# Eight units of attention instead of four ahead of the h stage, with the first W pairs among them and three w_out tiles decoded there

## The chip, the cores and the metric

The program runs on one core of one Trainium2 chip. The metric is the device time of the program in microseconds, as the median of several executions. A core has a matrix engine (TensorE, PE in the rows, with its weight loads as PEld), VectorE (DVE), ScalarE (ACT), GpSimd (POOL) and SyncE (SP), which here issues nearly all transfers; each runs its own instructions in a fixed order and waits for the others by semaphores.

## What is computed

```python
def sm_attn(qq, kk, vv):                      # per batch (8) and head (8)
    s = scale * qq @ kk.T                     # k, v: 576 x 64
    a = softmax(s)
    return a @ vv
p_packed = sm_attn(p, k, v)                   # p: 32 x 64, "packed" k and v
x = sm_attn(q, p_packed, p_packed)            # q: 576 x 64
x = x.transpose(0, 2, 1, 3).reshape(4608, 512)
h = x @ w_in                                  # 512 x 2048
g = s * relu(h) ** 2 + b
x2 = g @ w_out                                # 2048 x 512
y = ((x2 @ w1) * (x2 @ w2)) @ w3 @ w_out2     # 512 x 1024, 1024 x 1024, 1024 x 512
```

The weights w_in, w_out, w1, w2, w3 and w_out2 arrive as 64-bit floats, which the kernel decodes to 32 bit on the chip.

## The kernel before

Precision is kept by splitting each fp32 operand into a high and a low part; `mm3` (L84) multiplies by three matmuls (lines L85, L88, L89), and `split` (L76) makes the parts with a copy on ScalarE (L79) and a subtraction on VectorE (L82).

Decoding one 128 x 512 tile of 64-bit weights (class `Decode`, L121) takes one load into one of four raw buffers (L127, `RAWB` = 4), a square on ScalarE (L140) and four VectorE operations (L144, L150, L157, L161). The raw buffer is free again after L157.

The work on k, v and p is cut into 16 units, each of one batch and four heads. For a unit u, `load_k` and `load_v` (L282, L289) bring 576 KB each, into three buffers each; `A_tr` (L327) transposes k in four parts, `B_s1` (L343) makes the scores, `B_sm1` and `B_sm2` the softmax (L352 to L383), `C_tr` (L391) transposes it, `D_mm` (L406, L411) multiplies by v, and `D_ev` (L420, L421) puts the result into `ppT`. The buffer of k is free after the last transpose, that of v after `D_mm`.

The program has these stages. First a loop over units and tiles of w_in: in step i it loads and transposes unit i, does the scores of unit i-1, the softmax of i-2 and the values of i-3, and decodes three of the 16 tiles of w_in; from step 5 on it also works on the five tiles of q of batch 0 (`q_tr` L188, `q_sc` L202, `q_at` L236). Before the change this loop covers `N1` = 4 units. Then come eight steps of `W_pair` (L470), which multiply the results of batches 0 and 1 with w_in, with the rest of the q tiles; the first w_out loads and the stores of decoded w_in (`win_store`, L560) stand among them. Then the h stage begins: 256 steps idx over batch, half of the tokens and 16 blocks f of w_in's columns. `step_h` (6 matmuls of 288 columns, tile hps; relu and squares at L662 to L674) runs two steps ahead of `step_x` (12 matmuls, tiles xps), which takes w_out tile f. In the first 16 steps the kernel decodes w_out tile idx (`wo_dec`) just ahead of `step_x(idx)`.

The units that are not done in the first loop are spread over the h stage by `plan`, four at a time, so that a step gets at most two parts of a unit (`room`): units 4 to 7 from step 4, 8 to 11 behind them, 12 to 15 from step 98. These late parts use the same lines, save that the score softmax has two reductions (L363, L364). At step 46 the results of units 4 to 7 are wanted by `pp_split`. The last stage (w1, w2, w3, w_out2, lines prod and yps) is not touched.

The written order is only the start: a scheduler reorders instructions on each engine when the program is built, except those that are pinned. What stands in the program after that is shown with the change.

Of the kernel before, what the change touches and what calls it, by code (L numbers as in the profile page):

```python
# [22 lines left out]
def fused_kernel(  # L23
# [36 lines left out]
    NTILE = (NS + 1) // 2  # L60
# [3 lines left out]
    FB1 = F1 // P  # L64
# [101 lines left out]
    if True:  # L166
# [88 lines left out]


        NU = B * NG
        N1 = NU // 4
        ctx0 = ExitStack()
        a1 = ctx0.enter_context(pool("a1"))  # L260
        ctx1 = ExitStack()
# [242 lines left out]
        def wo_dec(f):  # L504
            d = wod.pop(f)
            d.square()
            d.bits1(pin=f == 2)
            d.bits2()
            if f >= NW // 2:
                wo_t[f] = sh.tile([P, 2, DM], F32R, tag="sh", name=f"wo{f}", bufs=NW // 2)  # L510
            else:
                wo_t[f] = wop[0].tile([P, 2, DM], F32R, name=f"wo{f}")
            split(wo_t[f][:, 0, :], wo_t[f][:, 1, :], d.f)
# [13 lines left out]
        def next_win():  # L527
            nonlocal nload
            if nload < NW:
                win_load(nload)  # L530
                nload += 1

        def decode_win():
            nonlocal nbit
            next_win()
            if nbit < NW:
                d = wd.pop(nbit)
                d.square()
                d.bits1(out=win_at(nbit).bitcast(I32))
                d.bits2()  # L540
                nbit += 1
# [1 line left out]
        load_k(0)  # L543
        load_p(0, pz_tile())
        next_win()
        next_win()
        load_k(1)
        next_win()
        make_identity(nc, ident)
# [9 lines left out]
            n = stores.pop(0)  # L559
            tc.keep_in_program_order(nc.sync.dma_start(out=win_d[n], in_=win_at(n)))  # L560

        AS = 5

        def q_step(jq, ps, part):
            if part == 0 and 0 <= jq < NTILE:
                q_tr(0, jq, ps("qtp"))
            if part == 1 and 0 <= jq < NTILE:
                q_sc(0, jq, ps("scp"))
                q_sm1(0, jq)
            if part == 2 and 0 <= jq - 1 < NTILE:  # L570
                q_sm2(0, jq - 1)
                q_ev(0, jq - 1, q_at(0, jq - 1, ps("atp")))

        for i in range(N1 + OFF):
            jq = i - AS
# [21 lines left out]
                A_tr(i, 3)  # L597
            if i >= OFF:
                D_ev(i - OFF)
            decode_win()  # L600
            if 2 <= i < N1 + 2:
                C_tr(i - 2, 0)
                C_tr(i - 2, 1)
            q_step(jq, q_ps, 2)
            if 2 <= i < 2 + NTILE:
                load_q(0, i - 2)
        for j in range(NW // 2):
            jq = j + N1 + OFF - AS
            q_step(jq, m_ps, 0)
            wps = q_ps if j % 2 == 0 else kt_ps  # L610
            W_pair(j, [wps("wps") for _ in range(2)])
            q_step(jq, m_ps, 1)
            q_step(jq, m_ps, 2)
            if j < 3:
                wo_load(j)
            elif j > 3:
                win_store()
                win_store()
        ctx0.close()
        ctx1.close()  # L620
        wop[0] = ctx_a.enter_context(pool("wop", "right"))


        ctx2 = ExitStack()
# [200 lines left out]

        def room(step):
            r_ = step % (2 * FB1) - 2
            return 2 - (step in wsteps) - (0 <= r_ < 5 * NTILE and r_ % 5 in (0, 1, 4))

        def plan(us, start):  # L830
            done = {("p", us[0]): start}
# [57 lines left out]
                    at(t, lambda u=u: D_ev(u))  # L889
            return s_  # L890

        end1 = plan(range(N1, N1 + 4), 4)
        end2 = plan(range(N1 + 4, N1 + 8), end1 + 5)
        end3 = plan(range(N1 + 8, NU), max(end2 + 5, 98))
        PPS = (46, 110, 172)
        assert all(e <= p_ for e, p_ in zip((end1, end2, end3), PPS)), (end1, end2, end3)


        def load_wo2(c):
# [30 lines left out]
                      w3T[m, half][:, 1].rearrange("p a b -> p (a b)"), ps)  # L930
        for idx in range(NST):
            n, r = divmod(idx, 2 * FB1)
            if idx + 3 < FB1:
                wo_load(idx + 3)
            for _ in range(2):
                if stores:
                    win_store()
            if idx < FB1:
                wo_dec(idx)
            if n + 1 < B and r == 2:  # L940
                extra = attn2_steps(n + 1)
            if idx in PPS:
# [288 lines left out]
```

## Time and profile before

| | |
|---|---|
| median of three runs | 1491.2 us (1488.91 to 1491.9) |
| profiled execution, its own time | 1486.73 us |
| span of the profiled execution | 1485.0 us |
| PE busy | 1434.2 us, 97% |
| PEld, DVE, ACT busy | 1314.9, 933.1, 674.1 us |
| data moved by DMA | 228.73 MB |

The page of the profile divides the span into 40 slices of 37 us. In the row of PE all slices but the first five show 9 tenths, the first shows 8 and the second 6. In the DMA row the first slice shows 9 tenths and the second 8. So the two ends of the program differ: up to about 91 us the engines wait for each other and for data; after about 160 us PE is busy without a break for hundreds of microseconds. The stage from 91.3 us on is h.

### The profile page before, as it was taken

To read this page: it belongs to the slowest core of one execution; us is meant where nothing else is said; L and a number is where in the kernel's file an instruction comes from. 1 tells how busy PE (TensorE), PEld (TensorE's weight loads), DVE (VectorE), ACT (ScalarE), POOL (GpSimd) and SP (SyncE) were. 2 spreads that over 40 slices of the span, in tenths; PEclk is the share of its full clock that TensorE was granted. 3 is DMA by queue.
4 is the path that set the end of the run, shared out by engine and by line. 5 is a ranking of instruction groups with operands and counts; after the bars stand their busy time and mean duration, and the time that the engine had idled before them with its cause. 6 is when DMAs were issued, how large, how long until landed. Compare 5 with 4: busy or idle time off the path is not lost.

```text
span 1485.0 us, 26189 instructions
## 1 busy us (share of the span) xinstructions
PE 1434.2 (97%) x10152; PEld 1314.9 (89%) x10152; DVE 933.1 (63%) x2078; ACT 674.1 (45%) x1565; POOL 3.5 (0%) x38
## 2 busy tenths in 40 slices
PE   8688999999999999999999999999999999999998
PEld 5268999999999899998899998899999999999997
DVE  5969644565556776658898564667575655756552
ACT  4456655776556775557776552122131211312111
POOL 0000000000000000000000000000000000000000
PEclk9689999999999999999999999999999999999999
DMA  9846331243235462534664551556565655555451
GB/s 249 260 149 194 107 82 47 58 115 95 77 114 159 123 173 79 148 104 145 193 200 157 177 178 44 211 192 242 179 213 173 215 194 170 194 179 188 171 170 43
DMA packets 127324, 228.73 MB, mean 154 GB/s; under 512 B 50912, under 2 KB 89824, under 8 KB 121056
## 3 DMA queue, kind: packets, MB, share of 16 engines
q1 hardware_dynamic: 127200, 227.06, 48.1%
q8 instruction: 80, 1.31, 0.4%
q14 instruction: 44, 0.36, 0.1%
HBM read 182.98 MB, written 44.04 MB: 153 GB/s over the span
## 4 chain that ended last, share of the span: by engine, by line
PE 48%; DMA 2%; DVE 2%; ACT 1%; issue 1%; SPq 0%; ACTq 0%; DVEq 0%
PE prod L85 8%; PE prod L89 8%; PE prod L88 8%; PE yps L88 4%; PE yps L89 4%; PE yps L85 4%; PE xps L85 2%; PE xps L88 2%; PE xps L89 2%; PE w4a L89 1%; PE w4a L85 1%; PE w4a L88 1%; PE hps L85 1%; PE hps L89 1%; PE hps L88 1%
## 5 line engine op out<-in xcount | busy, mean ns | idle before, releaser
L88 PE MATMUL xps<-gl,wo 128*128 128x288 f32 (+1 forms) x1024 | 301.1, 300 | 0.0
L89 PE MATMUL xps<-gh,wo 128*128 128x288 f32 (+1 forms) x1024 | 298.6, 298 | 0.0
L85 PE MATMUL xps<-gh,wo 128*128 128x288 f32 (+1 forms) x1024 | 274.3, 300 | 1.7 <-DVE wo L82 1.0
L85 PE MATMUL prod<-xc,whl 128*128 128x384 f32 x672 | 226.1, 336 | 2.5 <-DVE c L82 2.5
L89 PE MATMUL prod<-xc,whl 128*128 128x384 f32 x672 | 226.4, 337 | 0.0
L88 PE MATMUL prod<-xc,whl 128*128 128x384 f32 x672 | 226.2, 337 | 0.0
L88 PEld LDWEIGHTS xps<-gl,wo 128*128 128x128 f32 x1024 | 193.5, 189 | 4.5 <-issue 2.3
L89 PEld LDWEIGHTS xps<-gh,wo 128*128 128x128 f32 x1024 | 193.7, 189 | 2.4 <-issue 1.4
L85 PEld LDWEIGHTS xps<-gh,wo 128*128 128x128 f32 x1024 | 182.3, 189 | 6.5 <-issue 2.3
L662 ACT ACTIVATE r<-hps 128x288 f32<-128x288 f32 x256 | 104.4, 410 | 129.7 <-PE hps L89 128.3
L85 PE MATMUL hps<-ATh,wpl 128*128 128x288 f32 x512 | 155.8, 304 | 5.6 <-ACT r L662 4.2
L674 DVE TENSOR_TENSOR gl<-r,gh 128x288 fp32r<-128x288 f32 x256 | 115.1, 453 | 73.1 <-ACT gh L671 70.4
L89 PE MATMUL hps<-ATh,wph 128*128 128x288 f32 x512 | 153.8, 300 | 0.0
L88 PE MATMUL hps<-ATl,wph 128*128 128x288 f32 x512 | 153.5, 300 | 0.0
L85 PEld LDWEIGHTS prod<-xc,whl 128*128 128x128 f32 x672 | 126.2, 188 | 9.7 <-issue 2.8
L88 PEld LDWEIGHTS prod<-xc,whl 128*128 128x128 f32 x672 | 126.2, 188 | 8.2
L89 PEld LDWEIGHTS prod<-xc,whl 128*128 128x128 f32 x672 | 126.2, 188 | 0.1
L664 ACT ACTIVATE r<-r 128x288 f32<-128x288 f32 x256 | 112.6, 444 | 11.1 <-DVE gl L674 6.6
L88 PE MATMUL yps<-w,c 128*128 128x512 f32 x288 | 113.9, 396 | 0.0
L85 PE MATMUL yps<-w,c 128*128 128x512 f32 x288 | 113.2, 395 | 0.3 <-DVE c L82 0.3
L89 PE MATMUL yps<-w,c 128*128 128x512 f32 x288 | 113.4, 395 | 0.0
L85 PEld LDWEIGHTS hps<-ATh,wpl 128*128 128x128 f32 x512 | 97.2, 190 | 11.1 <-ACT r L662 6.4
(332 smaller groups left out, 2312.5 us busy)
## 6 DMA issues: line engine op xcount, KB each, us to landing
whl<-whl SPq DMA_DIRECT2D x48, 1792.0 KB, 7.2
raw<-in_moe_w_dram SPq DMA_DIRECT2D x32, 512.0 KB, 4.4
raw<-in_moe_w_out_dram SPq DMA_DIRECT2D x24, 512.0 KB, 4.6
x<-win SPq DMA_DIRECT2D x48, 256.0 KB, 2.7
v<-in_v_dram SPq DMA_DIRECT2D x16, 576.0 KB, 6.3
q<-in_q_dram SPq DMA_DIRECT2D x72, 128.0 KB, 4.4
x<-xst SPq DMA_DIRECT2D x16, 576.0 KB, 3.4
out_dram<-yst SPq DMA_DIRECT2D x72, 128.0 KB, 2.4
```

What stands on the lines that cost most here:

```text
L85: ins = nc.tensor.matmul(ps, wl, xh, start=start, stop=False)
L88: nc.tensor.matmul(ps, wh, xl, start=False, stop=False)
L89: nc.tensor.matmul(ps, wh, xh, start=False, stop=stop)
L662: nc.scalar.activation(r_, ps[:, :HS], AF.Relu)
L664: nc.scalar.activation(r2, r_, AF.Square)
L674: nc.vector.tensor_tensor(out=gl[:, :HS], in0=r2, in1=gh[:, :HS].bitcast(F32), op=ALU.subtract)
```

## The change

`N1` becomes 8, so units 4 to 7 are done in the first loop and only units 8 to 15 remain for the h stage (`plan` from step 20 and from step 98). The loop has eleven steps instead of seven; each decodes two w_in tiles instead of three, so all 16 are decoded by step 7. The second load and transposition of p move into the loop. From step 7 on (`WS`) each step carries two of the eight W pairs, so the separate loop of W pairs is gone. The first three w_out loads are issued in steps 8 to 10, eight w_in stores in steps 9 and 10; behind the loop three more w_out loads stand and the decoding of w_out tiles 0 to 2. In the h stage w_out tile idx+3 is decoded, and idx+6 loaded, at step idx. `room` gives no part of a unit to a step that has W work.

```diff
--- before.py
+++ after.py
@@ -255,7 +255,7 @@
 
 
         NU = B * NG
-        N1 = NU // 4
+        N1 = NU // 2
         ctx0 = ExitStack()
         a1 = ctx0.enter_context(pool("a1"))
         ctx1 = ExitStack()
@@ -504,7 +504,7 @@
         def wo_dec(f):
             d = wod.pop(f)
             d.square()
-            d.bits1(pin=f == 2)
+            d.bits1()
             d.bits2()
             if f >= NW // 2:
                 wo_t[f] = sh.tile([P, 2, DM], F32R, tag="sh", name=f"wo{f}", bufs=NW // 2)
@@ -542,7 +542,6 @@
 
         load_k(0)
         load_p(0, pz_tile())
-        next_win()
         next_win()
         load_k(1)
         next_win()
@@ -559,7 +558,7 @@
             n = stores.pop(0)
             tc.keep_in_program_order(nc.sync.dma_start(out=win_d[n], in_=win_at(n)))
 
-        AS = 5
+        AS, WS = 5, 7
 
         def q_step(jq, ps, part):
             if part == 0 and 0 <= jq < NTILE:
@@ -570,6 +569,10 @@
             if part == 2 and 0 <= jq - 1 < NTILE:
                 q_sm2(0, jq - 1)
                 q_ev(0, jq - 1, q_at(0, jq - 1, ps("atp")))
+
+        def w_pair(j):
+            wps = q_ps if j % 2 == 0 else kt_ps
+            W_pair(j, [wps("wps") for _ in range(2)])
 
         for i in range(N1 + OFF):
             jq = i - AS
@@ -597,28 +600,31 @@
                 A_tr(i, 3)
             if i >= OFF:
                 D_ev(i - OFF)
-            decode_win()
+            if i == 1:
+                load_p(1, pz_tile())
+            if i == 3:
+                p_tr(1, m_ps("ptp"), 2)
+            if i >= WS:
+                w_pair(2 * (i - WS))
             if 2 <= i < N1 + 2:
                 C_tr(i - 2, 0)
                 C_tr(i - 2, 1)
             q_step(jq, q_ps, 2)
+            if i >= WS:
+                w_pair(2 * (i - WS) + 1)
             if 2 <= i < 2 + NTILE:
                 load_q(0, i - 2)
-        for j in range(NW // 2):
-            jq = j + N1 + OFF - AS
-            q_step(jq, m_ps, 0)
-            wps = q_ps if j % 2 == 0 else kt_ps
-            W_pair(j, [wps("wps") for _ in range(2)])
-            q_step(jq, m_ps, 1)
-            q_step(jq, m_ps, 2)
-            if j < 3:
-                wo_load(j)
-            elif j > 3:
-                win_store()
-                win_store()
+            if N1 <= i < N1 + 3:
+                wo_load(i - N1)
+            if i > N1:
+                for _ in range(4):
+                    win_store()
         ctx0.close()
         ctx1.close()
         wop[0] = ctx_a.enter_context(pool("wop", "right"))
+        for f in range(3):
+            wo_load(f + 3)
+            wo_dec(f)
 
 
         ctx2 = ExitStack()
@@ -825,7 +831,7 @@
 
         def room(step):
             r_ = step % (2 * FB1) - 2
-            return 2 - (step in wsteps) - (0 <= r_ < 5 * NTILE and r_ % 5 in (0, 1, 4))
+            return 0 if step in wsteps else 2 - (0 <= r_ < 5 * NTILE and r_ % 5 in (0, 1, 4))
 
         def plan(us, start):
             done = {("p", us[0]): start}
@@ -889,11 +895,10 @@
                     at(t, lambda u=u: D_ev(u))
             return s_
 
-        end1 = plan(range(N1, N1 + 4), 4)
-        end2 = plan(range(N1 + 4, N1 + 8), end1 + 5)
-        end3 = plan(range(N1 + 8, NU), max(end2 + 5, 98))
+        end2 = plan(range(N1, N1 + 4), 20)
+        end3 = plan(range(N1 + 4, NU), max(end2 + 5, 98))
         PPS = (46, 110, 172)
-        assert all(e <= p_ for e, p_ in zip((end1, end2, end3), PPS)), (end1, end2, end3)
+        assert end2 <= PPS[1] and end3 <= PPS[2], (end2, end3)
 
 
         def load_wo2(c):
@@ -930,13 +935,13 @@
                       w3T[m, half][:, 1].rearrange("p a b -> p (a b)"), ps)
         for idx in range(NST):
             n, r = divmod(idx, 2 * FB1)
-            if idx + 3 < FB1:
-                wo_load(idx + 3)
+            if idx + 6 < FB1:
+                wo_load(idx + 6)
             for _ in range(2):
                 if stores:
                     win_store()
-            if idx < FB1:
-                wo_dec(idx)
+            if idx + 3 < FB1:
+                wo_dec(idx + 3)
             if n + 1 < B and r == 2:
                 extra = attn2_steps(n + 1)
             if idx in PPS:
```

What the program then holds, on three engines. SP's queue is the first (transfers in order of issue). Before the change, from a load of q on, through the last tile of w_in (raw_550) to the first of w_out:

```order
L174 DMA q_412<-in_q_dram 64x8x64 x2
L127 DMA raw_450<-in_moe_w_in_dram 128x512
L127 DMA raw_492<-in_moe_w_in_dram 128x512
L127 DMA raw_510<-in_moe_w_in_dram 128x512
L174 DMA q_529<-in_q_dram 64x8x64 x2
L127 DMA raw_550<-in_moe_w_in_dram 128x512
L174 DMA q_611<-in_q_dram 64x8x64 x2
L174 DMA q_686<-in_q_dram 64x8x64 x2
L302 DMA pz_1018<-in_p_dram 128x2x64 x2
L174 DMA q_751<-in_q_dram 64x8x64
L127 DMA raw_795<-in_moe_w_out_dram 128x512
```

With the change, from the k of unit 7 on:

```order
L282 DMA k_624<-in_k_dram 96x4x384
L127 DMA raw_586<-in_moe_w_in_dram 128x512
L174 DMA q_613<-in_q_dram 64x8x64 x2
L289 DMA v_740<-in_v_dram 96x4x384
L127 DMA raw_656<-in_moe_w_in_dram 128x512
L127 DMA raw_710<-in_moe_w_in_dram 128x512
L174 DMA q_737<-in_q_dram 64x8x64 x2
L289 DMA v_872<-in_v_dram 96x4x384
L127 DMA raw_778<-in_moe_w_in_dram 128x512
L127 DMA raw_832<-in_moe_w_in_dram 128x512
L174 DMA q_870<-in_q_dram 64x8x64
L127 DMA raw_1131<-in_moe_w_out_dram 128x512
```

The k and v loads of units 4 to 7 now all stand ahead of the last w_in tile (raw_832); the last three of the eight are seen here.

On VectorE before the change, the last softmax of q (E2_868, which PE transposes just ahead of h) and the first results of h (gh, gl):

```order
L215 TENSOR_TENSOR E2_868<-scp_861,mx2_866 64x256
L82 TENSOR_TENSOR ATl_837<-atp_875,ATh_836 128x2x128
L224 TENSOR_REDUCE mx2_866<-E2_868 64x8
L225 TENSOR_SCALAR mx2_866<-mx2_866 64x8
L226 RECIPROCAL mx2_866<-mx2_866 64x8
L227 TENSOR_TENSOR E2_868<-E2_868,mx2_866 64x256
L82 TENSOR_TENSOR ATl_837<-atp_895,ATh_836 128x2x64
L673 CAST gh_972<-r2_970 128x288
L674 TENSOR_TENSOR gl_973<-r2_970,gh_972 128x288
```

With the change (the last softmax of q is E2_1151), the end of the same stretch:

```order
L82 TENSOR_TENSOR wpl_1268<-wps_1282,wph_1267 128x512
L144 TENSOR_SCALAR x_1440<-raw_1314 128x512
L150 SCALAR_TENSOR_TENSOR x_1393<-raw_1302,x_1393 128x512
L226 RECIPROCAL mx2_1149<-mx2_1149 64x8
L82 TENSOR_TENSOR wo2_1335<-x_1330,wo2_1335 128x512
L82 TENSOR_TENSOR ATl_1119<-atp_1211,ATh_1118 128x2x128
L150 SCALAR_TENSOR_TENSOR x_1440<-raw_1314,x_1440 128x512
L157 SCALAR_TENSOR_TENSOR x_1393<-raw_1302,x_1393 128x512
L227 TENSOR_TENSOR E2_1151<-E2_1151,mx2_1149 64x256
L144 TENSOR_SCALAR x_1483<-raw_1326 128x512
L82 TENSOR_TENSOR wpl_1268<-wps_1261,wph_1267 128x512
L157 SCALAR_TENSOR_TENSOR x_1440<-raw_1314,x_1440 128x512
```

Operations on w_out (tiles x and wo, at L144, L150, L157, L161 and L82) stand between those of the softmax, and fourteen rows, nearly all of such operations, between its last one and the first gh.

PE around the first W pairs (wps) before the change; of the units only the values (pvp) and the result (ppp) of unit 3 are left:

```order
L406 MATMUL pvp_710<-v_415,E1T_675 32x64 x24
L188 MATMUL qtp_614<-ident_116,q_412 128x128 x4
L202 MATMUL scp_631<-ppT_139,qT_619 64x64 x8
L420 MATMUL ppp_737<-ident_116,pvx_735 128x128
L470 MATMUL wps_804<-winx1_147,ppT_139 64x512 x2
L188 MATMUL qtp_689<-ident_116,q_529 128x128 x4
L470 MATMUL wps_805<-winx1_147,ppT_139 64x512 x2
L202 MATMUL scp_696<-ppT_139,qT_694 64x64 x8
L188 MATMUL qtp_753<-ident_116,q_611 128x128 x4
L470 MATMUL wps_882<-winx3_149,ppT_139 64x512 x2
```

With the change:

```order
L470 MATMUL wps_1008<-winx1_147,ppT_139 64x512 x2
L343 MATMUL s1p_1017<-kT_874,pTd_497 32x288 x5
L202 MATMUL scp_916<-ppT_139,qT_899 64x64 x8
L470 MATMUL wps_976<-winx0_146,ppT_139 64x512 x2
L470 MATMUL wps_1009<-winx1_147,ppT_139 64x512 x2
L406 MATMUL pvp_1154<-v_740,E1T_1098 32x64 x12
L420 MATMUL ppp_1083<-ident_116,pvx_1081 128x128
L406 MATMUL pvp_1154<-v_740,E1T_1098 32x64 x12
L470 MATMUL wps_977<-winx0_146,ppT_139 64x512 x2
L391 MATMUL etp_1197<-ident_116,E1_1029 96x128 x3
L470 MATMUL wps_1122<-winx3_149,ppT_139 64x512 x2
L236 MATMUL atp_1003<-ident_116,E2_797 128x128 x2
```

The scores (s1p), transposes (etp) and values (pvp) of units 6 and 7 stand among the first W pairs (wps) and the q tiles.

## Rows read from the trace of the kernel before

**Rows 1.** Stages: span, busy us (count) of PE, PEld, DVE, ACT, POOL; PEclk, DMA share, GB/s
```profile
5.00:47.00 42.00, 32.57 (x365) 20.72 (x366) 27.40 (x63) 19.07 (x43) 0.26 (x6) 0.86 0.99 254
47.00:60.00 13.00, 7.58 (x47) 3.47 (x39) 12.63 (x29) 4.76 (x8) 0.00 (x0) 0.50 0.79 220
60.00:91.30 31.30, 22.46 (x136) 9.29 (x132) 23.49 (x57) 17.28 (x35) 0.00 (x0) 0.83 0.80 267
91.30:130.00 38.70, 36.09 (x267) 33.50 (x266) 30.50 (x70) 23.98 (x59) 1.58 (x16) 0.89 0.51 145
130.00:160.00 30.00, 25.55 (x239) 24.31 (x240) 28.93 (x71) 23.05 (x53) 0.99 (x10) 1.00 0.61 194
200.00:300.00 100.00, 100.00 (x876) 95.43 (x875) 48.19 (x123) 61.90 (x147) 0.00 (x0) 1.00 0.22 59
```

**Rows 2.** DMA issues, first 60 us: count, KB each, median us to landing
```profile
raw<-in_moe_w_in_dram SPq DMA_DIRECT2D x16, 512.0 KB, 7.4
k<-in_k_dram SPq DMA_DIRECT2D x4, 576.0 KB, 11.5
```

**Rows 3.** Timeline from last w_in load to first x: start us, us, engine, line, operation
```profile
52.96 0.55 SPq L127 DMA_DIRECT2D raw<-in_moe_w_in_dram  x1
59.54 0.43 DVE L144 TENSOR_SCALAR winx<-raw 128x512 int32<-128x512 int32 x1
...
91.33 0.61 PE L85 MATMUL hps<-ATh,wpl 128*128 128x288 f32 x1
...
96.50 0.71 PE L85 MATMUL xps<-gh,wo 128*128 128x290 f32 x4
```

**Rows 4.** Timeline, as before: starts of neighbouring instructions on VectorE and TensorE
```profile
66.62 0.41 DVE L224 TENSOR_REDUCE mx<-E 128x8 f32<-128x256 f32 x1
66.95 0.68 DVE L161 SCALAR_TENSOR_TENSOR winx<-m,winx 128x512 f32<-128x512 bf16 x1
...
101.10 0.30 PE L88 MATMUL hps<-ATl,wph 128*128 128x288 f32 x1
101.23 0.29 PE L89 MATMUL hps<-ATh,wph 128*128 128x288 f32 x1
...
104.17 1.28 DVE L157 SCALAR_TENSOR_TENSOR x<-raw,x 128x512 uint32<-128x512 uint32 x2
...
105.01 0.41 PE L327 MATMUL ktp<-ident,k 96*128 96x96 f32 x3
...
105.20 0.38 PE L85 MATMUL hps<-ATh,wpl 128*128 128x288 f32 x1
```

**Rows 5.** Groups on PE, 91.3 to 160 us: count, busy us, mean ns, idle before
```profile
L89 PE MATMUL xps<-gh,wo 128*128 128x290 f32 x64 | 19.6, 308 | 0.0
L89 PE MATMUL hps<-ATh,wph 128*128 128x288 f32 x46 | 14.4, 313 | 0.0
L327 PE MATMUL ktp<-ident,k 96*128 96x96 f32 x24 | 3.2, 250 | 0.0
L343 PE MATMUL s1p<-kT,pTd 64*32 64x288 f32 x16 | 1.4, 415 | 0.0
L406 PE MATMUL pvp<-v,E1T 96*32 96x64 f32 x48 | 1.2, 223 | 0.0
L391 PE MATMUL etp<-ident,E 128*96 128x128 f32 x6 | 1.0, 272 | 0.0
```

**Rows 6.** Waits of SP's queue, first 110 us: us, times, longest
```profile
SPq L127 <- DVE x L157: 18.0, 1, 18.0
SPq L174 <- PE qtp L188: 7.0, 1, 7.0
```

**Rows 7.** DMA issues of the whole program, w_out
```profile
raw<-in_moe_w_out_dram SPq DMA_DIRECT2D x24, 512.0 KB, 4.6
```

**Rows 8.** Waits of the engines, 59.5 to 91.3 us: us, times, longest
```profile
PE atp L236 <- DVE E L227: 3.8, 2, 2.5
ACT m L140 <- DMA raw<-in_moe_w_out_dram: 3.2, 2, 2.3
```


## The prediction

> **What bounds the kernel now.** I read the stages by time first [rows 1]. The reader should look at three of their columns: PE, DVE and the DMA share. From 5 to 47 us the DMA engines are busy 0.99 of the time at 254 GB/s while PE works 32.57 of 42.00 us and VectorE 27.40: transfers set the pace. From 47 to 60 us VectorE does (12.63 of 13.00). From 60 to 91.3 us nobody is full: PE 22.46, VectorE 23.49 of 31.30, TensorE's granted clock 0.83. From 91.3 us, where h begins, to 160 us VectorE is busy 30.50 + 28.93 = 59.4 of 68.7 us and PE loses time to it. By 200 us PE is busy 100.00 of 100.00, and work taken off PE there is time off the end. So the change moves units out of a stretch where PE is the bound into one where transfers are. The question is whether the first grows by less than the second shrinks.
>
> The timeline between the two gives the marks [rows 3]: the last w_in load is issued at 52.96, VectorE takes it up at 59.54, the first matmul of h starts at 91.33 and the first of x at 96.50.
>
> **Term 1: how much later h begins.** Ahead of the last w_in tile SP's queue holds, before, 8 loads of k and v at 576 KB, 16 of w_in at 512 KB [rows 2], 4 of q at 128 KB and 2 of p at 64 KB (sizes of the last two from the code): 13,440 KB. With the change it holds 16 of k and v, 16 of w_in, 8 of q and 4 of p: 18,688 KB. The difference is 5,248 KB or 5.37 MB. At the 254 GB/s of the stretch where the queue is full [rows 1] that is 21.2 us, at 267 GB/s 20.1 and at 220 GB/s 24.4. I take 21.2, the rate of the stretch with the same mix of loads. VectorE takes up the last w_in tile at 59.5 + 21.2 = 80.7 us. In that time VectorE has to do less than there is time for: four units add some ten short operations each and no decode.
>
> What follows the last tile is VectorE's. In the order, 52 rows of it lead from that tile's first operation to the last softmax operation of q, for which PE waits ahead of h. By kind: 25 operations on 512 columns, six L144, ten on about 256 columns, 11 short ones. Starts of neighbours tell what one costs in a full queue [rows 4]: two L157 take 1.28 us together where one takes 0.68, so 0.60 apart; a 256-wide one frees the engine after 0.33 (66.62 to 66.95), which I use for L144 too, and for a short one I estimate 0.2. The sum is 25 x 0.60 + 16 x 0.33 + 11 x 0.2 = 22.5 us. Before, the 58 rows of the same stretch come by the same prices to about 22.4 us, and took 91.3 - 59.5 = 31.8 us. The 9.4 us between are waits, such as PE's for the softmax (3.8) and ScalarE's for a w_out load (3.2) [rows 8], which come when VectorE has run out of other work; its busy 23.49 of 31.30 says so. Now three more w_out tiles stand there to fill such gaps, and six of the eight W pairs need no late tile. I take 1.8 us of waits, between none and 9.4. h begins at 80.7 + 22.5 + 1.8 = 105.0 us, against 91.3: **+13.7 us**.
>
> **Term 2: from the first h to the 160 us mark.** Up to 160 us PE did 3 x (64 + 46) = 330 matmuls of x and h [rows 5]; they start 0.13 apart where nothing holds them (101.10 and 101.23, [rows 4]); with 0.133 that is 43.9 us. Beside them it did parts of late units: two units' k transposes (24), one unit's scores (16), transposes (6) and values (48), and the second transposition of p. One unit's groups are busy 1.6 + 1.4 + 1.2 + 1.0 + about 0.3 (its transposed result) = 5.5 us [rows 5]; but matmuls overlap: after three transposes busy 0.41 us the next matmul starts 0.19 later [rows 4]. So a unit takes between 2.6 us (19 parts in 41 of it) and 5.5. I take 4.3, above the middle, since each change between kinds of matmul costs something too. The second unit's k transposes are 1.6 of 5.5, so 1.3 units were done: 5.6 us, with some 0.5 for p 6.1. The rest of the 68.7 us, 18.7, is q tiles, which stay, and waits.
>
> With the change the units and p go, -6.1 us. Of the waits I take 3.5 us away. The reason is VectorE: a w_out tile is four operations and a split, 4 x 0.60 + 0.33 = 2.7 us, and in the order five of the 16 tiles are finished and three more begun before the first gh, instead of two in all; four fewer tiles are 10.8 us out of 59.4, the units' own operations come on top, and in the first 16 steps VectorE stops being the bound. Against it, the 14 rows between the last softmax and the first gh (ten at 0.60, three at 0.33, 7.1 us) delay the first x: it starts some 7.5 us after the first h instead of 5.2, and PE idles there, since `step_h` is only two steps ahead. This is in the 3.5. **-9.6 us**, from -6 to -14.
>
> **Term 3: the units that no longer come after the mark.** Of units 4 to 7, 4 - 1.3 = 2.7 were done after 160 us, where PE is never idle [rows 1]: 2.7 x 4.3 = **-11.6 us**, from -7.0 to -14.9. VectorE, busy 48.19 of 100 there, covers its share of units 8 to 15 as before, and these only move to earlier or equal steps.
>
> The other edits I cost at nothing. Behind the last w_in tile SP's queue holds, up to the fifth w_out tile, five w_out loads (2.6 MB), eight w_in stores (2.1 MB) and five of q (0.7 MB): 5.4 MB, 20.2 us at the 267 GB/s of that stretch [rows 1]. VectorE wants that tile eight rows (3.5 us) ahead of the stretch's end, 22.5 - 3.5 + 1.8 = 20.8 us after the last w_in tile. So it covers them, but the cover is thin; without it the softmax waits, rival (b). ScalarE's part of an early unit, four copies of k, two of E1T and an exponential, lies beside the transfers (ScalarE 19.07 of 42.00 us). That a loop step decodes two w_in tiles and not three is hidden, since transfers set that pace.
>
> **Sum.** 1486.73 (profiled execution) + 13.7 - 9.6 - 11.6 = 1479.2 us. That execution lies 4.5 us under the median of 1491.2; on the median's footing the change gives **1483.7 us**, -0.5%. A measurement of this kernel can tell about 0.2%, 3 us, from no change.
>
> **Rivals.**
> (a) *The waits of the old tail come back.* The stretch of 31.8 us had 9.4 us of waits. If PE, ScalarE and VectorE hand the last q tiles to each other as slowly as before, h begins 7.6 us later: 1491.3 us, no change. For it: the last softmax chain is serial in both. Against it: VectorE has other work between now.
> (b) *Slower: w_out loads stand in front of the softmax.* Raw buffers are four. The fifth to seventh w_out load can be issued only after L157 of the tile four before, and VectorE's first operation on these tiles stands ahead of the last softmax (raw_1314, the fifth) and of the first gh (raw_1387, the seventh, raw_1434, the eighth). SP waited 18.0 us for such an L157 in one case [rows 6], and a w_out load takes 4.6 us from issue to landing [rows 7]. If each of three such round trips is exposed, 13.8 us are added: 1483.7 + 13.8 = 1497.5 us. It is slower than now by a measurable amount from about 10.5 us on, so two exposed trips (9.2) are not enough. Against it: the raw buffer of the first w_out tile is freed some 10 us before the fifth is wanted.
> The Trainium skill (DMA: Bandwidth & Descriptors, "Anatomy of one DMA") says that a wait of a transfer is spent on the issuing sequencer, so all that is queued behind it waits too; SP's 7.0 us for PE's q transposes [rows 6] agree.
> (c) *More is gained.* If k and v come at 267 GB/s (-1.1), h begins without waits (-1.8) and a unit costs 5.5 us on PE (4 x 1.2 = 4.8), the time is 1483.7 - 7.7 = 1476 us.
> (d) *The loads cost less.* k and v are read in runs of 1,536 bytes (6 x 64 x 4). If such runs moved faster than 254 GB/s and VectorE's decode of w_in had held them back, h would begin up to 8 us earlier and the time would be 1475 us. Against it stands the DMA share of 0.99. The Trainium skill (DMA: Bandwidth & Descriptors, "Specifications") calls 512 bytes enough for line rate and puts HBM's limit per core at about 358 GB/s; by that 5.37 MB would take 15.0 us instead of 21.2 and the sum would be 6 us lower. The row disagrees.
> (e) *It does not do what it says.* The scheduler could have put the units behind h again; the order excludes that, as s1p and pvp of units 6 and 7 stand among the first W pairs.
>
> **Chances.** The forecast, 1478 to 1488: 0.47. (a) 1488.5 to 1494: 0.19. (b) 0.16. (c) 0.14, (d) 0.04, (e) none. Faster by over 0.2% are the forecast, (c) and (d): 0.65; within 0.2% is (a): 0.19; slower is (b): 0.16. The range leaves out the farther half of (b) and the low end of (c) and (d): 1474 to 1496 us.
>
> **What would show it.** In the changed kernel's profile the DMA share should stay near 0.99 to about 78 us, VectorE's first operation on the last w_in tile should lie at 79 to 83 us, the first hps at 103 to 107, the first xps at 110 to 114. From the first h on, VectorE should no longer be over 85% busy, and L327, L343, L391 and L406 should have 48, 64, 24 and 192 fewer instructions behind h. The prediction is wrong if a DMA share well under 0.9 shows before 75 us (SP is held up), if VectorE waits over 5 us between the last w_in tile and the last softmax (a), or if L144 of w_out waits for its load there (b).

## The result, and the profile after

The changed kernel takes 1474.4 us (median of four runs, 1469.3 to 1478.5), the kernel before beside it 1491.0 us (1488.9 to 1491.9). The ratio is 0.989 with a 95% interval of 0.985 to 0.993: 16.6 us faster. The direction was right. The time lies below the 1478 to 1488 us that had the largest chance and just inside the wide range of 1474 to 1496 us; the gain forecast was 7.5 us. The profiled execution of the changed kernel took 1469.31 us, its span is 1467.5 us, 17.5 us under the span of before.

The first view is the one of [rows 1] with the same edges, for the changed kernel (span, busy us and count of PE, PEld, DVE, ACT, POOL; PEclk, DMA share, GB/s):

```profile
5.00:47.00 42.00, 36.69 (x373) 23.46 (x371) 25.55 (x60) 19.75 (x47) 0.00 (x0) 0.84 1.07 251
47.00:60.00 13.00, 10.25 (x137) 6.39 (x138) 8.68 (x27) 7.31 (x19) 0.26 (x6) 0.91 1.09 229
60.00:91.30 31.30, 28.27 (x352) 13.77 (x344) 25.91 (x70) 18.14 (x42) 0.00 (x0) 0.93 1.01 257
91.30:130.00 38.70, 29.30 (x184) 22.67 (x184) 38.70 (x90) 25.64 (x58) 1.17 (x12) 0.87 0.81 260
130.00:160.00 30.00, 30.00 (x249) 29.53 (x248) 27.61 (x67) 22.08 (x53) 1.47 (x14) 1.00 0.53 160
200.00:300.00 100.00, 100.00 (x932) 94.73 (x931) 44.65 (x116) 58.23 (x144) 0.00 (x0) 1.00 0.24 66
```

Against [rows 1], the DMA share stays over 1 up to 91 us, where it had fallen to 0.8 from 47 us on: the loads now set the pace that long. VectorE is busy all the time from 91.3 to 130 us. PE is full from 130 to 160 us, where it had lost 4.45 us.

The timeline of the changed kernel has the marks that answer [rows 3] (start us, us, engine, line, operation):

```profile
83.07 0.37 DVE L144 TENSOR_SCALAR winx<-raw 128x512 int32<-128x512 int32 x1
...
104.93 0.41 DVE L227 TENSOR_TENSOR E<-E,mx 64x256 f32<-64x256 f32 x1
...
108.61 0.27 DVE L82 TENSOR_TENSOR ATl<-atp,ATh 128x128 fp32r<-128x128 f32 x1
...
108.94 0.61 PE L85 MATMUL hps<-ATh,wpl 128*128 128x288 f32 x1 [2.13 <-DVE ATl L82]
...
113.36 0.29 PE L85 MATMUL xps<-gh,wo 128*128 128x290 f32 x1
```

The last w_in tile is taken up at 83.07 us (before 59.54), the first h starts at 108.94 (91.33), the first x at 113.36 (96.50).

Where the 17.5 us come from can be told by counting the matmuls of h and x, 4608 in both kernels, and reading when each number is reached. The table gives the time from one mark to the next, worked out from the records of the two traces; 18 matmuls are a step. Other work can cross a mark (12 W matmuls of steps 49 to 64 run behind matmul 1300 in the changed kernel alone), so single parts say less than the sums.

| part | steps | before | after | difference |
|---|---|---|---|---|
| to the first h | | 91.3 | 108.9 | +17.6 |
| h/x matmuls 1 to 337 | 0 to 19 | 68.7 | 50.6 | -18.1 |
| 337 to 1300 | 19 to 72 | 162.4 | 163.2 | +0.8 |
| 1300 to 2000 | 72 to 111 | 115.9 | 111.9 | -4.0 |
| 2000 to 2500 | 111 to 139 | 93.2 | 84.4 | -8.8 |
| 2500 to 4000 | 139 to 222 | 257.8 | 251.9 | -5.9 |
| 4000 to the end | | 695.7 | 696.5 | +0.8 |

Two things stand out. The first 19 steps gain twice what was forecast, and the rest comes in two places far behind them that the prediction does not name. At both, steps 113 to 128 and 177 to 192, the program computes `W_tile` for later batches ("W stretch" below).

### The profile page after: what moved, and what is told of

It is laid out like the page before. It is cut to its first block, busy times and chain, and to the rows that moved or that the text cites. A ratio compares the mean times of both kernels' runs of the same rounds, so it can differ in the third digit from the quotient of the medians.

```text
span 1467.5 us, 26161 instructions
## 1 busy us (share of the span) xinstructions
PE 1430.7 (97%) x10152; PEld 1310.6 (89%) x10152; DVE 931.2 (63%) x2070; ACT 669.4 (46%) x1557; POOL 3.6 (0%) x38
## 4 chain that ended last, share of the span: by engine, by line
PE 89%; DMA 7%; ACT 2%; DVE 2%; issue 1%; SPq 0%; ACTq 0%; DVEq 0%
PE xps L85 9%; PE xps L88 9%; PE xps L89 9%; PE prod L85 8%; PE prod L88 8%; PE prod L89 8%; PE yps L88 5%; PE yps L89 5%; PE yps L85 5%; PE hps L85 5%; PE hps L89 4%; PE hps L88 4%; DMA raw<-in_moe_w_in_dram 2%; DMA k<-in_k_dram 2%; PE scp L202 1%; PE qtp L188 1%
## 5 line engine op out<-in xcount | busy, mean ns | idle before, releaser
L88 PE MATMUL xps<-gl,wo 128*128 128x288 f32 (+1 forms) x1024 | 297.2, 298 | 0.0
L89 PE MATMUL xps<-gh,wo 128*128 128x288 f32 (+1 forms) x1024 | 295.5, 296 | 0.0
L85 PE MATMUL xps<-gh,wo 128*128 128x288 f32 (+1 forms) x1024 | 263.8, 299 | 0.1
L89 PEld LDWEIGHTS xps<-gh,wo 128*128 128x128 f32 x1024 | 192.9, 189 | 2.2 <-issue 1.4
L85 PEld LDWEIGHTS xps<-gh,wo 128*128 128x128 f32 x1024 | 178.2, 188 | 3.8 <-issue 0.9
```

The costliest lines, as they stand in the source:

```text
L85: ins = nc.tensor.matmul(ps, wl, xh, start=start, stop=False)
L88: nc.tensor.matmul(ps, wh, xl, start=False, stop=False)
L89: nc.tensor.matmul(ps, wh, xh, start=False, stop=stop)
```

## The experiments

All of them were compared with the kernel before on the same chip. A second number helps: from the first h on, kernels with the same order agree closely. The changed kernel took 1358.6 us from the first h to the end in its first trace and 1359.7 in another; before it was 1393.6. The first h itself moves by several microseconds from execution to execution, so this stretch shows more than the median does.

### The changed kernel again

No edit.

> The changed kernel once more, to see which of its gains repeat. In the first pair of profiles it was 17.7 us ahead at the end of the h and x matmuls, but level at h/x matmul 1300 (step 72); the 18 us came at matmuls 2000 to 2500 (W steps 113 to 128, -8.8 us, of which -5.2 us on the wps matmuls) and 3300 to 3500 (W steps 177 to 192, -5.6 us). Theory 'the plan does it': 1470 to 1479 us, and the wps matmuls at steps 113 to 128 again take about 0.23 us from one start to the next (0.33 in the kernel before). Theory 'chance of one execution': the time stays near 1474, but the wps matmuls of one of these stretches take 0.30 us or more in this profile.

Measured: 1476.0 us (1467.7 to 1476.9), ratio 0.989 (0.986 to 0.992). First h at 115.5 us instead of 108.9; from there every part of the table is within 1.1 us of the first trace (84.4 us for matmuls 2000 to 2500, wps 0.23 us apart). The gains behind the first h belong to the program; what changes between executions is when h begins. It goes with the rate of the loads. The windows from 5 to 83 us of the changed kernel in its two traces, and of the kernel without units 12 to 15 (below; same instructions up to h), in this order:

```profile
5.00:83.00 78.00, 67.50 (x772) 40.47 (x770) 51.83 (x136) 40.39 (x97) 0.26 (x6) 0.87 1.08 249
```
```profile
5.00:83.00 78.00, 62.83 (x711) 37.30 (x713) 45.45 (x117) 36.41 (x85) 0.26 (x6) 0.85 1.07 235
```
```profile
5.00:83.00 78.00, 63.94 (x640) 38.89 (x638) 42.33 (x109) 33.87 (x80) 0.26 (x6) 0.75 1.08 223
```

At one and the same DMA share the rate is 249, 235 and 223 GB/s, and the first h starts at 108.9, 115.5 and 120.3 us. From the start of the last VectorE operation on w_in to the first h it is 17.8 us in all three.

### The w_out part alone, and the units alone

The first is the kernel before with the w_out edits only, the second the changed kernel without them.

```diff
 # the kernel before, w_out part alone
-            d.bits1(pin=f == 2)
+            d.bits1()
...
+        for f in range(3):
+            wo_load(f + 3)
+            wo_dec(f)
...
-            if idx + 3 < FB1:
-                wo_load(idx + 3)
+            if idx + 6 < FB1:
+                wo_load(idx + 6)
...
-            if idx < FB1:
-                wo_dec(idx)
+            if idx + 3 < FB1:
+                wo_dec(idx + 3)
```

> The kernel before with the w_out part alone: three w_out tiles decoded ahead of h, the others three steps ahead of x; four units ahead of h as before. My forecast put the waits of VectorE and PE behind h at 3.5 us and the three decodes ahead of h at 15 VectorE rows, 6.5 us. Theory 'the w_out part takes the waits of the first 16 steps': h begins 5 to 8 us later, the first 16 steps lose 8 to 12 us, 1484 to 1489 us. Rival 'the waits are the late units' own': h begins 5 to 8 us later and gets back no more than that, 1490 to 1496 us.

> The changed kernel without the w_out part: eight units ahead of h, but every w_out tile decoded in its own step of x as before. Theory 'w_out takes the waits of the first 16 steps': h begins some 7 us earlier (101 to 103 us), PE waits for the w_out tiles behind it, end 1477 to 1484 us. Rival 'four late units fewer is all of it': h begins 7 us earlier and most of that stays, 1466 to 1473 us.

Measured: the w_out part alone 1492.4 us, ratio 1.002 (1.001 to 1.004); the units alone 1486.9 us, ratio 0.998 (0.996 to 1.000). Neither is worth anything to speak of; together they give 16.6 us. The w_out part alone came out in its rival's range, and yet the waits went, as its other theory has it; the units alone lie outside both ranges.

| | first h | h/x matmuls 1 to 337 | first h to end |
|---|---|---|---|
| before | 91.3 | 68.7 | 1393.6 |
| w_out part alone | 101.6 | 55.3 | 1388.9 |
| units alone | 104.0 | 66.9 | 1373.6 |
| both | 108.9 | 50.6 | 1358.6 |

The windows of these 336 matmuls, for the w_out part alone, the units alone and the changed kernel (the kernel before has, from 91.3 to 160 us, PE 36.09 + 25.55 and VectorE 30.50 + 28.93 busy of 68.7 us, [rows 1]):

```profile
101.60:156.90 55.30, 55.09 (x429) 52.86 (x429) 41.40 (x99) 37.70 (x93) 2.61 (x26) 0.97 0.51 155
```
```profile
104.00:170.90 66.90, 55.02 (x430) 52.49 (x431) 60.14 (x139) 43.24 (x100) 3.11 (x26) 0.97 0.50 156
```
```profile
108.90:159.60 50.70, 50.66 (x401) 49.95 (x402) 48.34 (x111) 37.13 (x88) 2.64 (x26) 0.97 0.60 192
```

With the units alone PE works 6.6 us less than before (55.0 against 61.6), which is close to the 6.1 us of the forecast, but it now stands still for 11.9 us instead of 7.1: VectorE's 60 us of work is there as before, and PE meets it sooner. Who is waited for is in PE's waits of that kernel over the same stretch:

```profile
PE xps L85 <- DVE wo L82: 7.1, 4, 3.2
PE hps L85 <- ACT r L665: 2.6, 2, 1.6
PE scp L202 <- ACT qT L194: 2.2, 1, 2.2
```

The w_out part takes VectorE's work there from 59.4 to 41.4 us, and PE waits no more; but ahead of h it must be done too. In the kernel before the loads of w_in are done by then, and the scheduler put eight w_out tiles ahead of the first h, which fill VectorE (busy 40.33 us of the 41.60 from 60 us to the first h): 10.3 us lost of the 13.4 gained, and of these only 4.7 are left at the end (1393.6 to 1388.9). In the changed kernel VectorE has time ahead of h while the loads run, and the same work costs 4.9 us (104.0 to 108.9) for 16.3 (66.9 to 50.6). Some of these differences of the first h are the loads' own, up to the 6.6 us seen between two traces of one kernel. The trace of the units alone is also that of its fastest execution of ten, 1479.4 us. An estimate by the medians takes from each median the time from the first h to the end and the 1.7 to 2.1 us by which the traced execution is longer than its span: the first h then starts at about 95.7 us before, 101.4 with the w_out part alone, 111.5 with the units alone and 114.0 with both. By this the w_out part costs some 6 us alone and 2 to 3 us beside the units.

### One w_out tile ahead, and three w_in tiles per unit

```diff
 # one tile ahead
-        for f in range(3):
-            wo_load(f + 3)
-            wo_dec(f)
+        wo_load(3)
+        wo_dec(0)
...
-            if idx + 6 < FB1:
-                wo_load(idx + 6)
+            if idx + 4 < FB1:
+                wo_load(idx + 4)
...
-            if idx + 3 < FB1:
-                wo_dec(idx + 3)
+            if idx + 1 < FB1:
+                wo_dec(idx + 1)
```

> The changed kernel with one w_out tile decoded ahead of h and the others one step ahead of x (instead of three and three). Theory 'the lead of one step is what matters, since PE then never meets a tile that is still being decoded': h begins 3 to 4 us earlier than in the changed kernel and the first 16 steps stay full, 1469 to 1474 us. Rival 'the number of decodes left for the first 16 steps matters: VectorE is the bound there': two tiles more, 10 VectorE rows, 4.3 us, come back, 1474 to 1480 us. If one step is too short, PE waits for wo again as it does without the w_out part (16 us more behind h): 1480 us or more.

Measured: 1478.3 us, first h to end 1360.1. The question stays unanswered, since the program hardly differs: the trace has the same 42 VectorE rows, one of them in another place, between the last w_in operation and the first h, three finished w_out tiles among them. The scheduler moves the decodes ahead by itself as far as loads and buffers allow.

```diff
 # three w_in tiles per unit
+            decode_win()
             if i == 1:
                 load_p(1, pz_tile())
```

> The changed kernel with three w_in tiles loaded and decoded per unit ahead of h instead of two, as the kernel before did: the same bytes, but the last w_in tile lands ahead of the k and v of units 6 and 7. Theory 'VectorE's tail behind the last load sets the first h': six VectorE rows (3 to 4 us) move from the tail into the stretch in which VectorE waits for loads, and h begins 3 to 8 us earlier; 1467 to 1473 us. Rival 'the last load sets it, whichever it is, and unit 7's own chain then ends last': within 2 us of the changed kernel, 1473 to 1477 us.

Measured: 1482.1 us (ten runs), some 7 us slower than the changed kernel, where either theory had it faster or level. The last w_in operation did come earlier (86.0 us against 91.2), but between it and the first h (116.1) stand 69 VectorE rows instead of 42: six w_out tiles are finished ahead of h instead of three. From the first h on it takes 1358.5 us, no less. So decodes beyond three ahead of h cost their VectorE time there and give nothing back, as the first 19 steps are full of PE's work already.

### Loads left out

```diff
+            if u > 5:
+                kt[u] = kt[5]
+                return
```

The same lines stand in the load of v; units 6 and 7 then work on the k and v of unit 5.

> The changed kernel without the loads of k and v for units 6 and 7, which take unit 5's tiles instead (so the third and fourth batches' output is not the reference's); every other instruction stays. It takes 4 x 576 KB = 2.36 MB out of the stretch ahead of h, where the DMA engines' share is 1.05 to 1.10 up to 83 us. Theory 'the loads set when h begins, VectorE's tail behind them is a constant': 2.36 MB at 233 to 247 GB/s is 9.6 to 10.1 us; the last w_in row and the first h both come that much earlier for the rate of that execution (after the rate of 247 GB/s at 99 us, after 208 to 221 GB/s at 110), the tail between them stays 17.8 us, and the median falls from 1474 to 1476 us to 1464 to 1467 us. Rival 'VectorE is nearly full there as well and takes over': the first h moves by 4 us or less, the tail grows by 5 us or more, 1470 to 1473 us.

Measured: 1470.3 us (1465.9 to 1474.5), 4 to 6 us less than the changed kernel, the time that the rival gave. Its windows behind 75 us:

```profile
75.00:83.00 8.00, 6.85 (x90) 3.05 (x86) 8.00 (x23) 6.48 (x15) 0.00 (x0) 1.00 0.68 241
83.00:106.80 23.80, 15.47 (x108) 5.38 (x108) 23.80 (x60) 14.40 (x30) 0.00 (x0) 0.83 0.87 265
```

The DMA share has fallen to 0.68 and VectorE is full from 75 us to the first h at 106.8, as the rival has it; but the stretch from the last w_in operation to the first h grew by 1.6 us only (17.8 to 19.4), where the rival had 5 us or more. By how much h itself moved this one trace can't tell, since the first h of the changed kernel lies between 108.9 and 115.5 us. By the medians two units' loads cost 4 to 6 us, not the 10 that their bytes take at the rate of the loads: VectorE's own work hides about half of them.

### What a late unit costs

```diff
-        end3 = plan(range(N1 + 4, NU), max(end2 + 5, 98))
+        end3 = 0
```

What needs `ppT` of batches 6 and 7 reads that of 4 and 5.

> The changed kernel with units 12 to 15 left out: no k, v or p loads, transposes, scores or softmax for them, and what needs their result takes that of units 8 to 11 (so the output of the last two batches is not the reference's). It prices a late unit. Theory 'a late unit costs its own matmuls': 12 ktp, 16 s1p, 6 etp, 48 pvp and 2 more rows are some 3.5 us of PE from start to start each in the changed kernel's trace, my forecast took 4.3: 4 units are 14 to 17 us, so 1457 to 1462 us. Rival 'a late unit costs what the change saved per unit behind the first h (35.3 us for four, 8.8 us each)': 1438 to 1443 us.

Measured: 1454.3 us; the first h came late (120.3 us), and from it to the end it is 1332.8 us, 25.8 less than the changed kernel, or 6.5 us a unit. That is more than the units' own matmuls (from start to start 12 transposes of k take 0.83 us, 16 matmuls of scores 1.24, 6 transposes 0.49, 48 of values 0.81 and the rest 0.1, 3.5 us in all, 14 for four), and less than 8.8. Of the 11.8 us beyond the 14, 9.8 lie between matmuls 3300 and 4000 (111.8 us instead of 121.6), around the third W stretch, where the changed kernel has no part of a unit; some 1.8 us of these 9.8 are six W matmuls and four q transposes that run ahead of matmul 3300 there. The measured price lies between the two theories.

### What crowds a W stretch

Four kernels move the late units about; the first number is where units 8 to 11 begin, the second where 12 to 15 begin (20 and 98 in the changed kernel).

```diff
 # 20 and 106
+        end3 = plan(range(N1 + 4, NU), max(end2 + 5, 106))
 # 45 and 106
+        end2 = plan(range(N1, N1 + 4), 45)
+        end3 = plan(range(N1 + 4, NU), max(end2 + 5, 106))
 # 4 and 45
+        end2 = plan(range(N1, N1 + 4), 4)
+        end3 = plan(range(N1 + 4, NU), max(end2 + 5, 0))
 # 20 and 81
+        end3 = plan(range(N1 + 4, NU), max(end2 + 5, 0))
```

A fifth, 20 and 114, also has the `room` of the kernel before.

> Units 12 to 15 start at step 106 as in the kernel before (not 98), all else as changed; unit 12 then spans steps 106 to 139 across the W steps 113 to 128. Theory 'the place of the third group gives the late gain': most of the 8.8 us of h/x matmuls 2000 to 2500 come back, 1480 to 1486 us. Rival 'the place of the group is worth nothing, only the number of late units counts': 1470 to 1479 us.

> The changed kernel with the third group of units started at step 114, and W steps allowed to take one part of a unit as in the kernel before: unit 12's transposes then stand among the W steps 113 to 128, where the kernel before has them by its trace (ptp and ktp at steps 117 to 122, since its second group runs late, to step 112). Theory 'late units that spill into a W stretch crowd its W matmuls together': the W matmuls begin later than step 119, take 0.30 us or more each instead of 0.23, and h/x matmuls 2000 to 2500 take 89 to 94 us instead of 84.4; 1479 to 1486 us. Rival 'the spill is harmless, the kernel before lost the 9 us by other things': 84 to 86 us there, 1470 to 1478 us.

> The changed kernel with units 8 to 11 started at step 45 and units 12 to 15 at step 106, where the kernel before has them: still four late units fewer, but the second group ends late again (its last ppp stands at step 112 in the kernel before, at 85 in the changed one). The stretch from the first h to the end is compared, since the first h itself moves with the loads from one execution to the next: 1358.6 to 1359.7 us in three traces of the changed kernel, 1393.6 before. Theory 'a group that ends late makes the W stretch behind it start late and crowds its W matmuls': wps of steps 113 to 128 again at 0.33 us or more (0.234 in the changed kernel), h/x matmuls 2000 to 2500 at 92 to 95 us (84.4), first h to end 1366 to 1371 us. Rival 'fewer late units is what opened that stretch': 84 to 86 us there, 1358 to 1362 us.

> The changed kernel with units 8 to 11 started at step 4 and units 12 to 15 right behind them (step 45, last part at step 101), so that no group ends shortly ahead of a W stretch that needs it. Theory 'late ends crowd the W stretches': the third stretch opens too (0.234 us per W matmul instead of 0.312, as in the run with units 12 to 15 left out, where h/x matmuls 3500 to 4608 took 161 us instead of 172), first h to end 1343 to 1353 us. Rival 'VectorE is full in the first 16 steps, and units there cost more than they give back': the first 16 steps take 55 us or more instead of 50.7 and the sum is within 5 us of the changed kernel, 1355 to 1364 us.

> The changed kernel with units 12 to 15 started right behind units 8 to 11 (step 81 instead of 98, last part planned at step 140 instead of 160), units 8 to 11 as changed. Theory 'late ends crowd the W stretches': the last ppp stands at 150 or earlier instead of 172, the third W stretch opens to 0.234 us per W matmul, first h to end 1346 to 1354 us; its rival, that the third stretch is crowded by other work (decodes, q steps), gives 1357 to 1361 us.

Measured medians: 1474.8, 1479.2, 1479.4, 1476.9 and 1472.4 us. By them none clearly beats the changed kernel (20 and 81 has 1466.3 to 1476.4 us, within that kernel's spread); the parts behind the first h say more. For each W stretch the table gives the step at which its first matmul (wps) really starts by the trace, the mean time from the start of one of its 48 wps matmuls to the start of PE's next matmul, and the time of the h/x matmuls around it.

| kernel | second stretch: step, ns, 2000 to 2500 | third: step, ns, 3300 to 4000 | first h to end |
|---|---|---|---|
| before | 124.8, 328, 93.2 us | 189.8, 330, 125.5 us | 1393.6 |
| changed | 119.0, 233, 84.4 | 186.6, 315, 121.6 | 1358.6 |
| 20 and 106 | 116.0, 235, 84.4 | 188.4, 353, 121.8 | 1358.7 |
| 20 and 114 | 116.5, 251, 84.8 | 189.7, 327, 125.8 | 1362.5 |
| 45 and 106 | 122.6, 249, 87.6 | 189.8, 333, 124.2 | 1362.3 |
| 4 and 45 | 126.0, 306, 93.5 | 180.3, 234, 111.8 | 1357.2 |
| 20 and 81 | 126.9, 321, 98.5 | 178.8, 233, 109.6 | 1359.3 |
| without 12 to 15 | 116.5, 236, 81.6 | 180.3, 234, 111.8 | 1332.8 |

Wherever a stretch begins, its last matmul starts within a few steps of the same place, at 135.8 to 139.0 in the second and 200.9 to 204.3 in the third, where the program has h take its results; what differs is when it begins. Begun early it costs 0.23 us a matmul; begun some six steps later, it costs 0.31 to 0.33 us, and PE runs ahead of ScalarE and VectorE, which must split each result. The windows of the second and third stretch show it, first of the kernel before, then of the one with 4 and 45:

```profile
477.40:531.30 53.90, 50.28 (x339) 45.76 (x338) 39.78 (x79) 41.81 (x91) 0.00 (x0) 0.97 0.52 146
681.00:738.40 57.40, 52.25 (x346) 45.58 (x345) 47.73 (x100) 45.83 (x101) 0.00 (x0) 1.00 0.53 164
```
```profile
496.40:548.00 51.60, 46.62 (x318) 41.60 (x315) 38.84 (x78) 40.76 (x89) 0.00 (x0) 1.00 0.48 140
659.00:726.80 67.80, 67.80 (x489) 64.74 (x488) 52.92 (x113) 54.46 (x122) 0.00 (x0) 1.00 0.46 142
```

and of the changed kernel:

```profile
458.20:520.00 61.80, 61.80 (x444) 58.66 (x444) 43.10 (x88) 48.54 (x105) 0.00 (x0) 1.00 0.46 140
657.70:718.90 61.20, 56.40 (x382) 50.19 (x380) 48.40 (x102) 48.38 (x107) 0.00 (x0) 1.00 0.49 154
```

An open stretch keeps PE busy without a gap (61.80 of 61.80, 67.80 of 67.80); a crowded one loses 3.6 to 5.2 us to waits. The granted clock is no rival for this: it is 1.00 in all but one of these windows, and the 0.97 of the second stretch of the kernel before is worth 0.03 of 53.9, 1.6 us, by estimate. In the second stretch of the kernel before it waits for this:

```profile
PE wps L85 <- ACT wpst L462: 2.9, 2, 2.4
PE hps L85 <- DVE wpl L82: 0.7, 1, 0.7
```

Each wps tile is held until ScalarE has copied it (L462), and there are only two such buffers, shared with the late units' parts and the q tiles.

Why a stretch begins late: the units' parts run behind the plan. In the kernel before the second group is planned to end at step 100, and its last result (ppp) stands at step 112 in the trace; the W matmuls planned for 113 begin at 125, as far behind. In the changed kernel the second group is over at step 85, and unit 12, planned to end at 112, ends at 117.7; the stretch begins at 119. Moving both groups early ("4 and 45", "20 and 81") opened the third stretch, as forecast, and crowded the second: units planned without a pause up to step 100 or 112 arrive at the second stretch some 14 steps late again. So the sums missed the forecast (1357.2 and 1359.3 us from the first h on, where 1343 to 1354 were given). "45 and 106" was to crowd the second stretch again, at 0.33 us or more, and did so by little, 0.249 us and 87.6 us, nearer to the rival that fewer late units open it. That their number alone does it is excluded by "4 and 45" and "20 and 81", which have as few as the changed kernel and are crowded there. That starting the third group at 98 instead of 106 gives the gain in the second stretch is excluded by "20 and 106" (84.4 us). That units merely stand among W matmuls is harmless: "20 and 114" has k transposes of unit 12 at steps 122 to 135 and 0.251 us a matmul, with 84.8 us around them. So my theory of that run was wrong: what it loses, it loses in the third stretch (125.8 us), which its later group crowds.

## Why the prediction came out as it did

**Term 1** was +13.7 and measured +17.6 in this pair of traces, with the loads at the upper end of their rates. Up to the last softmax operation it came out, in part by luck: the last w_in tile was taken up at 83.07 against 80.7 us, 2.4 late, but the 22.3 us from there to the end of that operation are the 22.5 of the rows alone, without the 1.8 of waits, so that it ended at 105.3 against 105.0. What failed is the step from there to h. The forecast let h begin with the end of the softmax, as it nearly does before, 0.5 us behind it; here h came 3.6 us behind it, the last 2.1 of them spent waiting for the split of the last transposed q tile (ATl, 108.61), ahead of which VectorE had five w_out operations and one of W to do. The kernel before starts h ahead of that split:

```profile
91.33 0.61 PE L85 MATMUL hps<-ATh,wpl 128*128 128x288 f32 x1
...
91.74 0.29 DVE L82 TENSOR_TENSOR ATl<-atp,ATh 128x128 fp32r<-128x128 f32 x1 [0.92 <-ACT ATh L79]
```

So the first h needs none of that tile's tokens. What it needs is the buffer: in the changed program as built, the first hps gets the PSUM bank (a buffer for results of matmuls) that the transposed tile had, bank 0, and its first matmul waits for that tile's split. In the kernel before that tile is in bank 3, with the units alone in bank 1, and there too h starts ahead of the split (104.00 and 104.15 us). By the medians the first h is 18.3 us later (95.7 to 114.0). Rivals (a) and (b) didn't come true: VectorE had no gap from 91.3 us to the first h. Rival (c), 1476 us, is nearest in time, but the loads didn't run at 267 GB/s and h didn't begin without a wait; only its dearer unit, 5.5 us, points the right way. Rival (d) fell too: with the queue full to 83 us the loads ran at 249 GB/s over that stretch here and slower elsewhere, not faster than the 254 assumed. The Trainium skill (DMA: Bandwidth & Descriptors, "Specifications") has 512 bytes enough for line rate, with some 358 GB/s as HBM's limit for a core; the rows here, with a mix of runs of 1,536 bytes (k, v) and 4 KB (w_in) and a share of 1.07 to 1.08, show 223 to 249 GB/s and disagree.

**Term 2** was -9.6, from -6 to -14, and measured -18.1. The mechanism, waits on VectorE that w_out decodes cause, was right; the term was mis-sized. I took 3.5 us of waits away, and all 7.1 went (PE 50.66 of 50.70 busy). And I counted a unit's parts by their own length, 6.1 us for 1.3 units; from start to start, with the waits that stood behind them, those rows (ktp, etp, s1p, pvp, ppp, ptp) took 10.9 us before and none now. The x and h matmuls took 5.2 us less (52.4 to 47.2), the q tiles' parts 2.0. A part of this is the granted clock, which the forecast left out: it was 0.89 from 91.3 to 130 us before and 0.97 over the 50.7 us after, which by estimate is (1 - 0.89) x 38.7 - (1 - 0.97) x 50.7 = 2.7 us. What I did not see is that units and w_out are not two terms to add: the units alone gave 1.8 us here.

The step that VectorE would "no longer be over 85% busy" was wrong: its work fell by 11.1 us, as worked out (10.8), but the stretch shrank by 18, and it is 95% busy (48.34 of 50.70).

**Term 3** was -11.6, from -7.0 to -14.9, behind the 160 us mark and measured -17.1, in another place. Up to matmul 1300 both kernels do three units, so nothing is gained there; the gain comes when the queue of units runs dry earlier: behind matmul 1300 the kernel before still finishes eight, the changed one five. Three units at 3.5 us are 10.5 of the 18.7 us gained between matmuls 1300 and 4000; the other 8 lie around the W stretches, which begin earlier: 5.3 of them are the W matmuls themselves, 48 x (0.328 - 0.233) + 48 x (0.330 - 0.315), and the rest isn't told apart. This second part is missing from the prediction: it held that late units only move to earlier or equal steps, and did not ask who waits for their end. That four late units take 6.5 us each (third group) and not 4.3 fits the same reason: without them the third stretch begins at step 180.3 and is open.

**The sum**: +17.6 - 18.1 - 17.1 = -17.6, with each term larger than forecast, the losses by 3.9 and the gains by 14. That the time still lies in the wide range, by 0.4 us, owes something to these misses offsetting each other.

Still open: why the units run behind the plan by as much as they do, and whether both stretches can be opened at once; no kernel here beats the changed one by more than the first h moves ("20 and 81": 1472.4 us, 1466.3 to 1476.4). An earlier place for the last ATl, or another bank for its tile, was not tried.

## What to carry to other kernels

Two edits that relieve two engines in one stretch must be priced together: taking 6.6 us of work off PE gave 1.8 us in a stretch where VectorE set the pace, and what was taken off VectorE there stood in its way ahead of that stretch. For work that is moved off a late queue, ask who waits for the queue's last item, and read from the trace, not from the plan, when that item comes. If the order is fixed from a point on, measure from that point to the end; it tells kernels apart that medians cannot.

## What the runs showed that was not expected

The same loads, at the same DMA share of 1.07 to 1.08, moved 223 to 249 GB/s in different executions, and the first h came between 108.9 and 120.6 us; behind it the time to the end repeats to about 1 us. The changed kernel, bound by loads for twice as long, carries this spread: 1467.7 to 1478.5 us in eight runs.
